# Block 0 of a state-space and gated feed-forward kernel: one copy moved to ScalarE, decay matmuls moved into two waits, loads placed anew

## The chip, the cores and the metric

The kernel runs on one core of a Trainium2 chip. The metric is the device time of one execution in microseconds. Engines are named as in the profile: PE is TensorE (matmul), PEld its weight loads, DVE is VectorE, ACT is ScalarE, POOL is GpSimd, SP is SyncE, which issues transfers.

## The reference

Two steps, the second on the result of the first. The first is a chunked linear recurrence over a sequence, for 4 batches x 8 heads, sequence 768, head size 32, state size 16:

```python
cum = np.cumsum(log_a)                       # within a chunk
M = (C @ B.T) * exp(cum_i - cum_j) * causal
y = M @ x + (C @ state) * exp(cum_i)
state = exp(sum(log_a)) * state + sum_j B_j x_j * exp(cum_last - cum_j)
```

The second takes y as 3072 tokens of 256 values, with weights of 256 x 1536 (gate and value) and 1536 x 256 (out):

```python
out = (np.maximum(y @ w_gate, 0.0) * (y @ w_val)) @ w_out
```

## The kernel before

The sequence of each batch is cut into chunks of 128 tokens, and two chunks are a pair: 12 pairs, three to a batch. The feed-forward step works on blocks of 512 tokens (two pairs): 6 blocks, NBLK. All is written in one order, and `in_order` (at the end) ties every engine to the order in which its instructions are written; each engine runs its own list and waits for the others by semaphores only.

A pair goes through these steps. The loads (`load`, or `held`, which first writes one element of the tile on DVE, so that the load isn't issued before DVE gets there) bring B, C and x. `dec_wide` makes the decay factors of a pair from the running products `cp`, by small fp32 matmuls; `late_decay` does so for pairs 2 and 3 into bank `d23`, and `decay` does all the others into `dall` (6 fp32 matmuls, L233), copied by ACT into `fac`. `scale` multiplies B by the reciprocal factors and C by the factors into `bs` (on POOL), and casts x into `xb`. `transp` (called through `turn`) transposes these on PE into `tp`; `bevac` and `cevac` (through `tevac`) copy out BT and two masked CT. `back` transposes BT back into bank `bt`, and `backevac` copies it to `bx`: B in the token order that the state needs. `G` makes C·B of the pair in four banks (8 matmuls, L364); `gevac` copies it to `gs` with the causal mask, partly by ACT casts (L377, L380) and POOL selects (L158), partly by DVE multiplies (L383, L385). `astep` adds one chunk to the state in `A_ps` (L397), and `sevac` copies it masked into `Sm` (L405). `inter` multiplies the state by C (L471) and `Dm` multiplies G by x (16 matmuls of 32 columns, L482), both into the bank of y (the tag `y`, of which there is one); `yevac` casts it into `yT`.

The feed-forward step has full tiles, `gv` (512 tokens of one of the NF = 12 slices of the hidden size: two matmuls for gate, two for value, ReLU on ACT at L514, product on DVE at L515 into `h`) and half tiles, `gvh` (256 tokens, L525, L528, L529), for which one pair's yT is enough. `fout` multiplies h by `wo` in four quarters of a block (L537), and `foevac` stores them. `keep_warm` writes filler matmuls of zeros into a tile of tag `y` that nobody reads.

G's four banks, bt, the tiles of gate and value, the output, `d23` and `dall` take turns in five shared PSUM banks (`bank`, NSHARED = 5): the n-th one waits until the (n-5)-th is copied out.

In block 0 nothing of the pairs ahead is ready, and the first pairs' steps stand between its half tiles. The order of before is half tiles 0 and 1 of pair 0's tokens, G and its copies, half tile 2, back and the copy bx on DVE, half tile 3, the decay of pairs 2 and 3, then `state`, `inter`, `Dm` and `yevac` of pair 1. The block's loop goes on with half tiles 4 and 5 of the first tokens, 0 to 5 of the second, and full tiles 6 to 11, with pair 2's steps between them, and `decay` at its end. The weights' slices 8 to 11 and `wo` are loaded by POOL's queue just ahead of half tile 3.

Of the kernel before, what the change touches and what calls it, by code (L numbers as in the profile page):

```python
# [29 lines left out]
def kernel(  # L30
# [35 lines left out]
    def bank(name="bank", shape=(128, 512), dtype=FP32):  # L66
        return mm.tile(list(shape), dtype, tag="shared", bufs=NSHARED, name=name)
# [174 lines left out]
    def new_bs(p):  # L242
        st[p]["bs"] = att.tile([128, 4, 128], BF16, tag="bs", name="bs", bufs=6)
        bs = st[p]["bs"]
        if p < NWIDE:
            st[p]["tin"] = [[bs[:, 2 * j + r] for r in range(2)] for j in range(2)]
        else:
            st[p]["tin"] = [[bs[:, 2 * i + j] for i in range(2)] for j in range(2)]
            st[p]["B"] = st[p]["tin"][0]
# [43 lines left out]
    def scale(p, eng):  # L293
        new_bs(p)
        scale_bc(p, eng)
        to_x(p, eng)
# [55 lines left out]
    def backevac(p, eng):  # L352
        s = st[p]
        bx = att.tile([128, 2, 128], BF16, tag="bx", name="bx", bufs=4)
        copy(eng, bx, s.pop("bt"))
        s["B"] = [bx[:, i] for i in range(2)]
# [44 lines left out]
    def sevac(p, i):  # L401
        if 2 * (p % PPB) + i == NC - 1:
            return
        S[2 * p + i + 1] = n = att.tile([128, 2, 128], BF16, tag="Sm", name="Sm", bufs=5)
        nc.vector.tensor_tensor(out=n, in0=A_ps[0], in1=smask, op=ALU.mult)  # L405

    def state(p, i):
        astep(p, i)
        sevac(p, i)
# [51 lines left out]
    def inter(p, i):  # L461
        s = st[p]
        y_bank(s)
        if 2 * (p % PPB) + i == 0:
            return
        Sm = S.pop(2 * p + i)
        for t in range(2):
            out = s["y"][t][:, i]
            if p < NWIDE:
                out = out.rearrange("s (r m) -> s r m", r=2)  # L470
            nc.tensor.matmul(  # L471
                out=out, lhsT=Sm[:, t], rhs=ct(p, i, t=t),
                start=opening(s, t), stop=False, skip_group_check=True)

    def Dm(p, apart=False):
        s = st[p]
        y_bank(s, apart)
        for t in range(2):
            for i in range(2):
                new = opening(s, t)  # L480
                for q in range(4):
                    nc.tensor.matmul(  # L482
                        out=s["y"][t][32 * q:32 * q + 32, i],
                        lhsT=s["x"][i][:, (4 * t + q) * D:(4 * t + q + 1) * D],
                        rhs=s["gs"][:, q, 2 * i + t],
                        start=new, stop=True,
                        tile_position=(0, 32 * q), skip_group_check=True)

    def yevac(p, *engs):
        s = st.pop(p)  # L490
        dst = yT[:, :, p * 256:(p + 1) * 256]
        if p >= NWIDE:
            copy(engs[0], dst.rearrange("q t (i m) -> q t i m", i=2), s["ya"])
            return
        for t in range(2):
            copy(engs[t % len(engs)],
                 dst[:, t].rearrange("q (i m r) -> q i r m", i=2, r=2),
                 s["y"][t].rearrange("q i (r m) -> q i r m", r=2))
# [15 lines left out]
        nc.scalar.activation(r, g, AF.Relu)  # L514
        nc.vector.tensor_tensor(out=fst[b][:, f], in0=r, in1=v, op=ALU.mult)  # L515

    def gvh(b, f, u):
        if f == 0 and u == 0:
            fst[b] = ffn.tile([128, NF, 512], BF16, tag="h", name="h")
        tk = slice(b * 512 + u * 256, b * 512 + (u + 1) * 256)  # L520
        fs = slice(f * 128, (f + 1) * 128)
        gv_ = bank("gv", (128, 2, 256))
        for j, w in ((0, wg), (1, wv)):
            for k in range(2):
                nc.tensor.matmul(out=gv_[:, j], lhsT=w[:, k, fs], rhs=yT[:, k, tk],  # L525
                                 start=(k == 0), stop=(k == 1), skip_group_check=True)
        r = ffn.tile([128, 512], BF16, tag="r", name="r", bufs=3)[:, 0:256]
        nc.scalar.activation(r, gv_[:, 0], AF.Relu)  # L528
        nc.vector.tensor_tensor(out=fst[b][:, f, u * 256:(u + 1) * 256], in0=r,  # L529
                                in1=gv_[:, 1], op=ALU.mult)  # L530

    def fout(b, ts):
        if ts % 2 == 0 or b == NBLK - 1:
# [48 lines left out]
    keep_warm(3)  # L582
    astep(0, 0)
    sevac(0, 0)
    new_bs(1)
    scale_bc(1, nc.vector, C_)

    def held(p):

        new_bc(p)  # L590
        nc.vector.memset(st[p]["bcr"][0:1, 0, 1, 0, 0:1], 0.0)
        load(p, nc.sync)
# [14 lines left out]
    def late_decay():  # L607
        d = bank("d23", (128, 2, 2, 8))
        for p in (2, 3):
            dec_wide(d[:, p - 2], p, p == 2)  # L610
        nc.scalar.copy(out=wfac[:, 2:4, 1], in_=d)
        nc.vector.reciprocal(wfac[:, 2:4, 0], d)

    def decay():
        d = bank("dall", (128, HC, 2, NB, 8))
        dec_all(d, range(HC))
        for w in range(2):
            cs = slice(w * HC, (w + 1) * HC)
            nc.scalar.copy(
                out=fac[:, :, cs, 1, :].rearrange("p b k h -> p k b h"), in_=d[:, :, w])  # L620
# [16 lines left out]
    gvh(0, 1, 0)  # L637
    G(1)
    gevac(1)
    gvh(0, 2, 0)  # L640
    back(1)
    backevac(1, nc.vector)
    weights(8, NF)
    weights_out(0, NF)
    gvh(0, 3, 0)
    late_decay()
    state(1, 0)
    inter(1, 0)
    inter(1, 1)
    Dm(1)  # L650
    state(1, 1)
    yevac(1, nc.scalar)

    for b in range(NBLK):
        P, Q, W = 2 * b + 2, 2 * b + 3, 2 * b + 1
        more = P < NPAIR
        for n in (P + 2, P + 3):
            if b and n < NPAIR:
                load(n, nc.sync)

        nh = 6 if b < 2 else 5
        for f in range(nh):
            if b == 0 and f < 4:
                continue
            gvh(b, f, 0)
            if b and f == (4 if b == 1 else 2):
                inter(W, 0)
                inter(W, 1)
                Dm(W)
                if b > 1 and more:  # L670
                    states(P)
                yevac(W, nc.scalar)
                if b > 1 and more:
                    spread(P)
        for f in range(nh):
            gvh(b, f, 1)
            if b == 1 and f in (0, 3):
                scale(P if f == 0 else Q, nc.gpsimd)
        for f in range(nh, NF):
            gv(b, f)  # L680
            if b == 0:
                if f == 6:
                    scale(P, nc.gpsimd)
                    for n in (3, 4, 5):
                        held(n)
                if f == 8:
                    turn(P)
                    tevac(P, nc.scalar, nc.vector)
                if f == 9:
                    back(P)  # L690
                    backevac(P, nc.vector)
                if f == 10:
                    state(P, 0)
                if f == 11:
                    scale(Q, nc.gpsimd)
                    state(P, 1)
            elif more:
                if f == (6 if b == 1 else 5):
                    turn(P)
                    tevac(P, nc.scalar, nc.vector)  # L700
                    if b > 1:
                        scale(Q, nc.gpsimd)
                if f == (9 if b == 1 else 8):
                    turn(Q)
                    tevac(Q, nc.scalar, nc.vector)
                    if Q + 1 < NPAIR:
                        scale(Q + 1, nc.gpsimd)
        if b == 0:
            decay()
        if more and b != 1:  # L710
            inter(P, 0)
            inter(P, 1)
        fout(b, 0)
        foevac(b, 0)
        if b == 1:
            states(P)
        if more:
            G(P)
        if b == 1:
            spread(P)  # L720
        if more:
            gevac(P)
        if b == 0:
            turn(Q)
            tevac(Q, nc.scalar, nc.vector)
        fout(b, 1)
        foevac(b, 1)
        if b == 0:
            back(Q)
            backevac(Q, nc.vector)  # L730
            for n in range(NB):
                nc.vector.reciprocal(fac[:, n, :, 0], fac[:, n, :, 1])
        fout(b, 2)
        foevac(b, 2)
        if more:
            if b == 1:
                inter(P, 0)
                inter(P, 1)
            Dm(P)
            states(Q)  # L740
            yevac(P, nc.scalar)
            G(Q)
            spread(Q)
            gevac(Q)
        fout(b, 3)
        foevac(b, 3)
# [32 lines left out]
```

## Time and profile before

| | |
|---|---|
| median of 3 runs | 131.5 us (131.4 to 131.59) |
| the profiled execution | 131.41 us, its span 129.7 us |
| busy: PE, DVE, ACT, POOL | 122.8, 94.1, 78.7, 42.3 us |
| half tile's matmul, 128x256, at 12 us and at 15 us | 421 ns, 272 ns |
| `dall`'s 6 matmuls | 28.19 to 29.07 us |
| first output matmul (L537) | 29.24 us |

Times in the profile are microseconds from the start of the span. A line of a timeline has the start, the time from first to last end, the engine, the line of the kernel, the operation and its tiles, the count, and in brackets how long the engine was idle before and who released it. The chain of work that ended last has the start, the length and the work, each piece being the one that the next one waited for.

### The profile page before, as it was taken

The page shows a single profiled execution, that of the slowest core. Times are in us where ns is not written, and L with a number is a line of the kernel's source. Part 1 is how long each engine was busy: PE and PEld are TensorE (multiplying, and loading weights), DVE is VectorE, ACT ScalarE, POOL GpSimd, SP SyncE. Part 2 cuts the span into 40 slices and gives each one's busy share as a digit, 9 for nine tenths or more (in the row PEclk, how much of TensorE's full clock was granted, in tenths as well). Part 3 has the DMA queues.
Part 4 walks back from the last instruction along what each step waited for, and adds up shares of the span by engine and source line. Part 5 has one row for each costly group of instructions (what it writes and reads, how often), then busy time and mean ns, then how long its engine had stood idle before and what let it go on. Part 6 is the DMA issues. An engine that isn't in the chain of part 4 may idle for free.

```text
span 129.7 us, 3374 instructions
## 1 busy us (share of the span) xinstructions
PE 122.8 (95%) x1253; PEld 84.9 (65%) x1260; DVE 94.1 (73%) x226; ACT 78.7 (61%) x175; POOL 42.3 (33%) x79
## 2 busy tenths in 40 slices
PE   6999879999999999999999999999999999999990
PEld 2555568547787557887467885477885577864770
DVE  4668769883986987579974888965898866597410
ACT  4062648744588864488744788745887645886410
POOL 7997392016193053261403523102800032000000
PEclk9999999999999999999999999999999999999999
DMA  3999999997999697259940289832200002200031
GB/s 70 146 185 161 175 134 145 190 156 79 121 117 214 70 130 110 81 107 120 110 73 0 86 133 134 95 55 81 81 5 0 0 0 86 81 0 0 5 104 58
DMA packets 71152, 11.98 MB, mean 92 GB/s; under 512 B 64864, under 2 KB 71072, under 8 KB 71136
## 3 DMA queue, kind: packets, MB, share of 16 engines
q1 hardware_dynamic: 63408, 8.49, 42.0%
q0 software_dynamic: 5360, 2.75, 16.6%
q10 hardware_dynamic: 2368, 0.52, 2.3%
q8 instruction: 10, 0.16, 0.5%
q14 instruction: 6, 0.05, 0.1%
HBM read 11.11 MB, written 3.15 MB: 110 GB/s over the span
## 4 chain that ended last, share of the span: by engine, by line
PE 84%; POOL 6%; DVE 4%; issue 2%; ACT 0%; POOLq 0%; DVEq 0%
PE o L537 25%; PE gv L525 22%; PE val L511 13%; PE gate L508 12%; PE y L482 4%; PE g L364 3%; PE tp L310 2%; PE y L471 2%; POOL bcr L86 1%; DVE h L515 1%; DVE gs L383 1%; POOL xb L168 1%; DVE h L529 1%; POOL wg L143 1%; PE A_ps L428 1%
## 5 line engine op out<-in xcount | busy, mean ns | idle before, releaser
L537 PE MATMUL o<-wo,h 128*128 128x256 bf16 x288 | 34.3, 273 | 0.0
L515 DVE TENSOR_TENSOR h<-r,val 128x512 bf16<-128x512 bf16 x40 | 27.3, 685 | 5.7 <-ACT r L514 2.2
L529 DVE TENSOR_TENSOR h<-r,gv 128x256 bf16<-128x256 bf16 x64 | 26.7, 421 | 6.1 <-ACT r L528 5.3
L537 PEld LDWEIGHTS <-h 128*128 128x128 bf16 x288 | 27.2, 98 | 5.3 <-issue 1.9
L514 ACT ACTIVATE r<-gate 128x512 bf16<-128x512 f32 x40 | 23.9, 597 | 8.1 <-PE gate L508 7.3
L528 ACT ACTIVATE r<-gv 128x256 bf16<-128x256 f32 x64 | 24.6, 384 | 4.2 <-PE gv L525 1.8
L525 PE MATMUL gv<-yT,wg 128*128 128x256 bf16 x128 | 25.1, 277 | 0.5 <-DVE h L529 0.5
L158 POOL TENSOR_SCALAR_AFFINE_SELECT gs<-gs 128x512 bf16<-128x512 bf16 (+1 forms) x24 | 12.2, 531 | 41.0 <-ACT gs L377 41.0
L525 PE MATMUL gv<-yT,wv 128*128 128x256 bf16 x128 | 24.9, 277 | 0.0
L511 PE MATMUL val<-yT,wv 128*128 128x512 bf16 x80 | 23.8, 379 | 0.3
L508 PE MATMUL gate<-yT,wg 128*128 128x512 bf16 x74 | 22.5, 379 | 0.0
L383 DVE TENSOR_TENSOR gs<-g,masks 128x512 bf16<-128x512 f32 x24 | 15.4, 684 | 5.4 <-PE g L364 5.4
L511 PEld LDWEIGHTS <-wv 128*128 128x128 bf16 x80 | 7.8, 98 | 9.4
L525 PEld LDWEIGHTS <-wg 128*128 128x128 bf16 x128 | 12.3, 99 | 2.6 <-issue 0.8
L525 PEld LDWEIGHTS <-wv 128*128 128x128 bf16 x128 | 12.7, 99 | 1.9 <-issue 0.2
L278 POOL TENSOR_TENSOR bs<-bcr,fac 128x256 bf16<-128x256 f32 x16 | 9.6, 620 | 12.0 <-DMA bcr<-in_B_dram 8.3
L252 ACT CAST yT<-y 128x512 bf16<-128x512 f32 (+1 forms) x15 | 7.4, 521 | 9.9 <-PE y L482 5.2
L377 ACT CAST gs<-g 128x512 bf16<-128x512 f32 x12 | 7.1, 589 | 8.9 <-PE g L364 8.9
L508 PEld LDWEIGHTS <-wg 128*128 128x128 bf16 x80 | 7.4, 98 | 5.6
L439 DVE TENSOR_TENSOR Sm<-A_ps,smask 128x256 bf16<-128x256 f32 x15 | 5.7, 415 | 6.5 <-PE A_ps L428 6.5
L553 ACT COPY ob<-o 128x512 f32<-128x512 f32 x10 | 5.9, 585 | 4.7 <-PE o L537 4.7
L252 POOL CAST xb<-xr 128x512 bf16<-128x512 f32 x11 | 6.8, 615 | 5.5 <-DMA xr<-in_x_dram 5.5
(79 smaller groups left out, 106.1 us busy)
## 6 DMA issues: line engine op xcount, KB each, us to landing
xr<-in_x_dram SPq DMA_DIRECT2D x21, 128.0 KB, 3.4
out_dram<-ob SPq DMA_DIRECT2D x10, 256.0 KB, 2.2
bcr<-in_C_dram SPq DMA_DIRECT2D x16, 64.0 KB, 3.1
bcr<-in_B_dram SPq DMA_DIRECT2D x16, 64.0 KB, 2.9
wg<-in_moe_w_gate_dram POOLq DMA_DIRECT2D x3, 256.0 KB, 4.4
wv<-in_moe_w_val_dram POOLq DMA_DIRECT2D x3, 256.0 KB, 4.8
wo<-in_moe_w_out_dram POOLq DMA_DIRECT2D x1, 768.0 KB, 9.8
bcr<-in_C_dram SPq DMA_DIRECT2D x3, 128.0 KB, 4.1
```

The lines of the kernel that those rows point to most:

```text
L158: nc.gpsimd.affine_select(out=dst, in_=dst, pattern=pattern, compare_op=ALU.is_ge, fill=0.0, base=0, channel_multiplier=-1)
L252: (eng.copy if eng is nc.scalar else eng.tensor_copy)(out=out, in_=in_)
L278: eng.tensor_tensor(out=dst[:, :, t], in0=src[:, :, t], in1=f[:, :, 4 * t:4 * t + 4].to_broadcast([128, n, 4, N]), op=ALU.mult)
L383: nc.vector.tensor_tensor(out=d[:, q], in0=g[q], in1=m, op=ALU.mult)
L508: nc.tensor.matmul(out=g, lhsT=wg[:, k, fs], rhs=yT[:, k, tk], start=(k == 0), stop=(k == 1))
L511: nc.tensor.matmul(out=v, lhsT=wv[:, k, fs], rhs=yT[:, k, tk], start=(k == 0), stop=(k == 1))
L514: nc.scalar.activation(r, g, AF.Relu)
L515: nc.vector.tensor_tensor(out=fst[b][:, f], in0=r, in1=v, op=ALU.mult)
L525: nc.tensor.matmul(out=gv_[:, j], lhsT=w[:, k, fs], rhs=yT[:, k, tk], start=(k == 0), stop=(k == 1), skip_group_check=True)
L528: nc.scalar.activation(r, gv_[:, 0], AF.Relu)
L529: nc.vector.tensor_tensor(out=fst[b][:, f, u * 256:(u + 1) * 256], in0=r, in1=gv_[:, 1], op=ALU.mult)
L537: nc.tensor.matmul(out=o[:, ts % 2], lhsT=fst[b][:, f, ts * 128:(ts + 1) * 128], rhs=wo[:, f], start=(f == 0), stop=(f == NF - 1), skip_gr ...
```

## The change

It is all in block 0. The copy `bx` of pair 1 goes from DVE to ACT, right behind G's casts. Half tiles 2 and 3 are split in two functions, so that their matmuls come ahead of pair 1's state step and their ReLU and product behind it. `decay` moves from the end of the block to the wait between pair 1's state and D, and its bank from the shared ones to the tag `tp`; `late_decay` moves behind D of pair 1, and the reciprocal is taken from the copied factors. Pair 1's yT is cast by ACT and DVE, one half each. The block has 4 half tiles for each pair and 8 full ones, in place of 6 and 6. Pair 2's scaling, transposes and state step come earlier, and loads 3, 4 and 5 are held at three places instead of one. Nine filler matmuls of 128 columns stand between pair 0's state step and its D.

```diff
+    def gvh_mm(b, f, u):            # the matmuls of gvh
...
+        fst[b, f, u] = gv_
+
+    def gvh_evac(b, f, u):          # ReLU and product of gvh
+        gv_ = fst.pop((b, f, u))
...
     astep(0, 0)
     sevac(0, 0)
+    keep_warm(9, 128)
     new_bs(1)
     scale_bc(1, nc.vector, C_)
...
         nc.scalar.copy(out=wfac[:, 2:4, 1], in_=d)
-        nc.vector.reciprocal(wfac[:, 2:4, 0], d)
 
     def decay():
-        d = bank("dall", (128, HC, 2, NB, 8))
+        d = mm.tile([128, HC, 2, NB, 8], FP32, tag="tp", name="dall")
...
     G(1)
     gevac(1)
-    gvh(0, 2, 0)
     back(1)
-    backevac(1, nc.vector)
+    backevac(1, nc.scalar)
+    gvh_mm(0, 2, 0)
+    gvh_mm(0, 3, 0)
     weights(8, NF)
     weights_out(0, NF)
-    gvh(0, 3, 0)
+    astep(1, 0)
+    sevac(1, 0)
+    gvh_evac(0, 2, 0)
+    decay()
+    inter(1, 0)
+    Dm(1)
+    inter(1, 1)
+    astep(1, 1)
+    yevac(1, nc.scalar, nc.vector)
+    gvh_evac(0, 3, 0)
     late_decay()
-    state(1, 0)
-    inter(1, 0)
-    inter(1, 1)
-    Dm(1)
-    state(1, 1)
-    yevac(1, nc.scalar)
+    held(3)
+    nc.vector.reciprocal(wfac[:, 2:4, 0], wfac[:, 2:4, 1])
+    sevac(1, 1)
+    scale(2, nc.gpsimd)
...
-        nh = 6 if b < 2 else 5
+        nh = (4, 6, 5)[min(b, 2)]
         for f in range(nh):
-            if b == 0 and f < 4:
+            if b == 0:
                 continue
...
             if b == 0:
+                if f in (5, 7):
+                    held(4 if f == 5 else 5)
                 if f == 6:
-                    scale(P, nc.gpsimd)
-                    for n in (3, 4, 5):
-                        held(n)
-                if f == 8:
                     turn(P)
                     tevac(P, nc.scalar, nc.vector)
-                if f == 9:
+                if f == 7:
                     back(P)
                     backevac(P, nc.vector)
-                if f == 10:
+                if f == 9:
                     state(P, 0)
-                if f == 11:
                     scale(Q, nc.gpsimd)
+                if f == 10:
                     state(P, 1)
...
-        if b == 0:
-            decay()
```

More of the change, by code (lines that the diff above doesn't have):

```diff
@@ L515, in gv @@
         nc.vector.tensor_tensor(out=fst[b][:, f], in0=r, in1=v, op=ALU.mult)
-    def gvh(b, f, u):
+    def gvh_mm(b, f, u):
         if f == 0 and u == 0:
@@ L530, in gvh @@
                                 in1=gv_[:, 1], op=ALU.mult)
+    def gvh(b, f, u):
+        gvh_mm(b, f, u)
+        gvh_evac(b, f, u)
     def fout(b, ts):
@@ L681 @@
             if b == 0:
+                if f in (5, 7):
+                    held(4 if f == 5 else 5)
                 if f == 6:
-                    scale(P, nc.gpsimd)
-                    for n in (3, 4, 5):
-                        held(n)
-                if f == 8:
                     turn(P)
                     tevac(P, nc.scalar, nc.vector)
-                if f == 9:
+                if f == 7:
                     back(P)
                     backevac(P, nc.vector)
+                if f == 9:
+                    state(P, 0)
+                    scale(Q, nc.gpsimd)
                 if f == 10:
-                    state(P, 0)
-                if f == 11:
-                    scale(Q, nc.gpsimd)
                     state(P, 1)
```

## The prediction

> **What bounds the kernel now.** I read the page first (busy time, then the slices), then the chain that ended last in order of time, then PE's timeline from 8 to 30 us, with ACT's and DVE's beside it, and last the transfers.
>
> ```profile
> PE 122.8 (95%) x1253; PEld 84.9 (65%) x1260; DVE 94.1 (73%) x226; ACT 78.7 (61%) x175; POOL 42.3 (33%) x79
> ```
>
> TensorE is the bound, with little left where it is full. So I looked for the stretch in which the chain leaves it:
>
> ```profile
> 10.43 0.87 PE y L482 x14
> ...
> 12.33 1.72 PE gv L525 x8
> 14.07 0.39 ACT r L528
> 14.49 0.42 DVE h L529
> 14.91 1.20 DVE gs L383 x2
> 16.11 0.33 DVE gs L385
> 16.44 0.33 DVE h L529
> 16.77 0.20 DVE bx L252
> 16.97 0.33 DVE h L529
> 17.30 0.27 DVE wfac L612
> 17.57 0.29 DVE Sm L405
> 17.90 0.28 PE y L471 x2
> ...
> 28.26 0.81 PE dall L233 x6
> ```
>
> From 14.07 to 17.90 the end is set by ACT and DVE, one instruction after the other: DVE masks G of pair 1 and does everything else behind it, the copy bx among it. From 18.5 on the chain is PE's almost throughout; there a step counts by its PE time, and `dall` is 0.81 us of it. PE's timeline shows the rest:
>
> ```profile
> 10.43 0.87 PE L482 MATMUL y<-gs,xb 128*32 128x128 bf16 x16 [0.19 <-POOL gs L158]
> ...
> 13.40 0.63 PE L525 MATMUL gv<-yT,wv 128*128 128x256 bf16 x2
> 13.97 0.52 PE L364 MATMUL g<-CT,BT 32*128 32x256 bf16 x8
> 14.96 0.38 PE L525 MATMUL gv<-yT,wg 128*128 128x256 bf16 x2 [0.48 <-DVE h L529]
> ...
> 27.12 0.28 PE L397 MATMUL A_ps<-xb,bx 128*128 128x256 bf16 x1 [0.23 <-DVE bx L252]
> ```
>
> Two matmuls of 128x256 take 0.63 us at 13.40 and 0.38 us at 14.96. In a run of them one starts every 0.213 us before 13.8 and every 0.109 us after: TensorE's pace doubles between 13.6 and 14.0, though the page's clock row stands at full for the whole span. That is about 3.5 us after D of pair 0 began at 10.43, and since then PE hardly paused.
>
> **The change, part by part.** The sum is made against the profiled execution: 131.41 us, of which 129.70 are the span; the runs' median is 131.5, 0.09 above.
>
> *The nine filler matmuls ahead of D of pair 0.* They write the tag-y bank that D's output also uses, so D waits for the last one. The first can start at about 10.16 (the filler before ends at 10.02, and D's weight load then started at 10.16). Cold 128-column fillers start 0.107 us apart: 0.96 us. The last takes 0.31, and with the same 0.14 D starts at 11.5, not 10.43. Its data are then all there: 11 of its matmuls took 0.44 us from 10.79 on, so 16 take 0.6, and inter follows at 12.1 instead of 11.23.
>
> What the fillers can bring is the pace. Before, PE stood from 10.02 to 10.43; now matmuls follow one another from the three fillers at 8.53 on. If the pace doubles 3.5 us after the start of an unbroken run, that is 12.0. I take this, since it is the only interval the trace shows. Then inter is done at about 12.3, the two casts at 12.78 (now 12.11, so +0.67), and the eight gv matmuls take 0.87 instead of 1.70. G of pair 1 is no longer behind them but behind DVE: Sm 0.41 and CT 0.61 after the cast (13.75), then h of the first half tile, whose bank G's fourth quarter takes (14.15). G ends at 14.55, against 14.49. The fillers and the faster pace cancel up to here.
>
> *bx on ACT.* ACT casts two parts of G (0.58 and 0.38) from 14.5 and copies bx at 15.45 to 15.83 (0.38, the row of BT). Now bx ends on DVE at 16.96. DVE's masking runs from 14.6 to 16.2, against 14.83 to 16.43.
>
> *Half tiles 2 and 3, A, decay, D, late decay.* PE's order becomes gv2, gv3, A, dall, inter, D, inter, A, d23. gv2 needs the bank of the first G quarter (15.1). gv3 needs that of the second, which DVE's last masking frees at 16.2; A, with bx ready, is queued behind gv3. So gv3 runs 16.25 to 16.69 (0.44 for a half tile), A to 16.80, dall (0.81) to 17.6, and Sm on DVE (17.05 to 17.4) hides under dall, where now PE waits 0.48 for it. Then 0.11 inter, 0.34 D, 0.11 inter, 0.11 A: 18.28. d23's 16 matmuls (16.16 to 16.83 now, in a wait) take 0.67: 18.95. The two casts of yT, split over ACT and DVE, need 0.22 + 0.45 after the second inter (18.85), so d23 covers them; without it PE would wait 0.6. The stream of gate and value tiles starts at 18.95 instead of 18.57: +0.38.
>
> *The stream.* Now 8 half tiles and 6 full ones (0.437 and 0.863 each: 8.67 us), after it 4 and 8 (8.65). dall is out of it: -0.81. Its work with turn, back and A (0.45) would end 9.12 after 18.57, at 27.69, but dall started at 28.19: 0.5 us stands idle, most of it at A of pair 2, which waited for bx. With turn two tiles and back two tiles earlier, bx is some 0.6 us ahead of A, and this goes: -0.5, with 0 as the other end if DVE falls behind. The last value tile's h must be done before the last matmul of the first output quarter, 1.2 us after it starts; relu and h take 1.3 from the last gate, so it is just hidden, where now dall gives 0.8 more room.
>
> *The loads and small steps.* Load 3 moves from 24.3 to about 19.6, 4 and 5 to two points of the stream. SP issues them and does nothing else then. The scaling of pair 2 moves behind the reciprocal (0.35 on DVE): POOL does it by 21.7 (1.2 and 0.6), and turn needs it at 23.3. The two fac copies on ACT (0.38) fall before yT's casts are ready. Zero for all these; the loads' risk is a rival.
>
> Sum: +0.38 - 0.81 - 0.5 - 0.02 = -0.95 us: 130.46, so 130.5. Behind block 0 nothing is changed and PE stays full; the gain should reach the end whole.
>
> **The rivals.**
>
> *The pace doubles no earlier than now.* If it is not the unbroken run that counts but fixed stretches of time, one ends near 13.9, and the one before it ended near 10.5, where only 0.35 us of the fillers have yet run. For it: eight fillers from 1.26 to 4.64 were an unbroken run of 3.4 us too, and the pace stayed. Price: gv runs from 12.98 cold until 13.9 and ends at 14.4, G ends at 14.97, masking at 16.7, gv3 at 17.2, and the stream starts at 19.45 (+0.88): 131.41 + 0.88 - 1.33 = 130.96, so 131.0. If, on the contrary, the stretch ending at 10.5 now passes, yT comes at 12.24, masking ends at 15.8, the stream starts at 18.53: 130.0.
>
> The Trainium skill, page "TensorE: Matmul & The Clock Gate", Part 1, "What's actually happening", says that the gate is opened by a busy window of about 3.4 us and that this window runs freely, not from the first matmul. By that page the fillers could bring nothing or the whole; the trace's eight early fillers agree that 3.4 us of matmuls alone are not enough.
>
> *The later stretch fails too.* D now comes after a pause of 0.4 us for the fillers' bank. If this keeps the pace low until 17.3, gv and G cost 0.5 more than in the rival above: 131.5.
>
> *wo comes late (the slower end).* This is the transfer in question, with the load that now starts beside it:
>
> ```profile
> wo<-in_moe_w_out_dram POOLq DMA_DIRECT2D x1, 768.0 KB, 9.8
> 24.34 0.37 SPq L86 DMA_DIRECT2D bcr<-in_C_dram  x1
> ```
>
> wo was issued at 17.50 and landed at 27.3; the first output matmul started at 29.24, and by the sum it starts at 28.3. Load 3 (0.52 MB) was issued at 24.34, beside wo's end; now it runs beside wo's whole length. At the 168 GB/s that the queues moved between 21 and 27 us, all of it ahead of wo is 3.1 us: landing at 30.4, a stall of 2.1, and 132.6. It decides from a landing later than 28.3. Against it: the wv part issued at 11.46 had load 2 beside it from 11.7 on and took 4.5 us, in the 4.5 to 5.0 of the others.
>
> **How the numbers follow.** Early pace, 130.0 to 130.8: 0.48. Pace as now, 130.8 to 131.4: 0.26. Both late, 131.5: 0.06. wo late, 131.8 to 132.8: 0.12. The rest, 0.08, is a price wrong by over 0.5 us that I do not see, mostly upwards, as the order on PE is now tight from 15 us on. A measurement of this kernel tells about 0.2%, 0.26 us, from no change: faster means below 131.24. From the first case 0.47 and from the second 0.14 lie there, with a trace of the rest: 0.62. Slower is above 131.76: wo late and the most of the rest, with the late pace's tail: 0.22. Between: 0.16. Range 129.9 to 132.1: it leaves out the far part of wo's delay and the lowest corner of the first case. The first case's own range is 130.0 to 130.8.
>
> **What would show it.** Right: 128x256 matmuls at 0.109 us apart by the first gv; bx on ACT by 15.9; Sm (L405) released with no PE wait, dall in its place; no PE wait for bx near A of pair 2; the first output matmul near 28.3. Wrong: gv of pair 0 still at 0.213 us (the fillers cost 1 us and bring nothing), a PE wait of the output matmul for wo, or a wait of gv3 longer than that for masking.

## The result, and the profile after

The changed kernel takes 129.69 us (4 runs, 129.5 to 130.14) against 131.51; the ratio is 0.9867, interval 0.984 to 0.9894. It is faster, by 1.8 us where 0.95 to 1.0 were forecast, and lies 0.2 below the range. Later runs of the kernel before lie in two groups with medians of 130.5 and 131.4; the first four all fell in the upper one. Why there are two is half of what follows. All medians and ranges from here on leave out disturbed runs, over 1.5% longer than the fastest of their kernel.

The busy times on the page after: TensorE has 1.5 us less work in a span 1.8 us shorter, so its share is as before.

```profile
PE 121.3 (95%) x1261; PEld 83.7 (65%) x1261; DVE 94.3 (74%) x224; ACT 78.5 (61%) x173; POOL 42.7 (33%) x79
```

The chain that ended last, after, over the stretch shown of before (start, length, work):

```profile
9.89 1.07 POOL gs L158 x2
11.68 0.44 PE tp L310 x4
12.54 0.61 DVE CT L332 x2
13.90 0.58 ACT gs L377
14.53 1.03 PE gv L525 x8
15.67 0.81 PE dall L233 x6
17.29 0.46 ACT yT L252
17.76 0.46 DVE yT L252
18.26 1.80 PE gv L525 x15
...
27.64 1.31 PE o L545 x12
```

The row of DVE pieces from 14.49 to 17.90 is gone: the chain crosses from ACT's cast of G to PE at 14.53, and `dall` stands in it at 15.67 in place of 28.26. PE's timeline, after:

```profile
8.16 0.81 PE L193 MATMUL w<-warm 128*128 128x512 bf16 x3
...
9.44 0.67 PE L193 MATMUL w<-warm 128*128 128x128 bf16 x9
10.64 0.71 PE L482 MATMUL y<-gs,xb 128*32 128x128 bf16 x16 [0.53 <-POOL gs L158]
...
12.04 0.38 PE L525 MATMUL gv<-yT,wg 128*128 128x256 bf16 x2
...
15.60 0.88 PE L233 MATMUL dall<-pick,cp 64*128 64x64 f32 x6
16.41 0.29 PE L471 MATMUL y<-CT,Sm 128*128 128x128 bf16 x2
...
25.41 0.27 PE L397 MATMUL A_ps<-xb,bx 128*128 128x256 bf16 x1
...
27.47 1.47 PE L545 MATMUL o<-wo,h 128*128 128x256 bf16 x12
```

Three things are to be seen. The first gv pair takes 0.38 us and not 0.63, so the pace was high before it; the three 512-column fillers at 8.16, ahead of everything that the change touches, already start 0.216 us apart (0.427 before). D of pair 0 at 10.64 waits for POOL, not for the nine fillers, which end at 10.11. And the state step of pair 2 (25.41) no longer waits for bx. The first output matmul starts at 27.47 against 29.24, 1.77 us earlier; from it to the end of the span it is 100.46 us in both.

### The profile page after: what moved, and what is told of

It reads as the page before. It is cut to its first block, busy times and chain, and to the rows that moved or that the text cites. A ratio compares the mean times of both kernels' runs of the same rounds, so it can differ in the third digit from the quotient of the medians.

```text
span 127.9 us, 3378 instructions
## 1 busy us (share of the span) xinstructions
PE 121.3 (95%) x1261; PEld 83.7 (65%) x1261; DVE 94.3 (74%) x224; ACT 78.5 (61%) x173; POOL 42.7 (33%) x79
## 4 chain that ended last, share of the span: by engine, by line
PE 86%; POOL 7%; issue 2%; DVE 1%; ACT 1%; POOLq 0%; DVEq 0%
PE o L545 25%; PE gv L525 21%; PE gate L508 14%; PE val L511 14%; PE y L482 3%; PE g L364 3%; PE tp L310 2%; PE y L471 2%; POOL wg L143 1%; POOL bcr L86 1%; POOL xb L168 1%; POOL gs L158 1%; PE A_ps L428 1%; PE dall L233 1%; POOL ident masks.py:199 1%
## 5 line engine op out<-in xcount | busy, mean ns | idle before, releaser
L515 DVE TENSOR_TENSOR h<-r,val 128x512 bf16<-128x512 bf16 x42 | 28.7, 686 | 5.6 <-ACT r L514 2.5
L514 ACT ACTIVATE r<-gate 128x512 bf16<-128x512 f32 x42 | 25.1, 597 | 8.2 <-PE gate L508 7.4
L533 DVE TENSOR_TENSOR h<-r,gv 128x256 bf16<-128x256 bf16 x60 | 25.1, 421 | 5.0 <-ACT r L532 4.1
L532 ACT ACTIVATE r<-gv 128x256 bf16<-128x256 f32 x60 | 23.1, 385 | 3.4 <-DVE wfac L666 0.6
L508 PE MATMUL gate<-yT,wg 128*128 128x512 bf16 x84 | 25.0, 379 | 0.0
L511 PE MATMUL val<-yT,wv 128*128 128x512 bf16 x84 | 25.0, 379 | 0.0
L525 PE MATMUL gv<-yT,wg 128*128 128x256 bf16 x120 | 23.3, 273 | 0.4 <-ACT gs L377 0.2
L525 PE MATMUL gv<-yT,wv 128*128 128x256 bf16 x120 | 22.9, 272 | 0.0
L511 PEld LDWEIGHTS <-wv 128*128 128x128 bf16 x84 | 8.2, 98 | 9.9
L525 PEld LDWEIGHTS <-wv 128*128 128x128 bf16 x120 | 11.7, 98 | 1.8 <-issue 0.5
L525 PEld LDWEIGHTS <-wg 128*128 128x128 bf16 x120 | 11.2, 98 | 2.2 <-issue 0.6
L508 PEld LDWEIGHTS <-wg 128*128 128x128 bf16 x84 | 7.8, 98 | 6.2
```

What stands on the lines that cost most here:

```text
L508: nc.tensor.matmul(out=g, lhsT=wg[:, k, fs], rhs=yT[:, k, tk], start=(k == 0), stop=(k == 1))
L511: nc.tensor.matmul(out=v, lhsT=wv[:, k, fs], rhs=yT[:, k, tk], start=(k == 0), stop=(k == 1))
```

## The experiments

Medians are of 5 to 12 runs. `before` ran beside each group, with medians of 131.0 to 131.4.

**When does the pace double?** Both kernels were profiled again, and the nine fillers were taken from the one and given to the other.

> The kernel before, unchanged, profiled a second time. The question is when TensorE's pace doubles, and whether that moment moves from run to run. Theory A (fixed stretches of 3.4 us that run freely, and a stretch counts or not by how full it is): the moment lies anywhere between about 6.5 and 14 us, and differs from the first profile's 13.9; where it is near 7, D of pair 0 still starts near 10.4 because it waits for POOL, and the time is 0.3 to 0.7 us less than 131.4. Theory B (an unbroken run of matmuls decides): 13.9 again, 131.4 to 131.6.

Measured: 131.37 us (130.35 to 131.94), in two groups. The profile by stretches (ends of the stretch, its length, PE's busy time and instructions, granted clock, DMA):

```profile
core 0: us, PE busy (x), PEclk, DMA share, GB/s
0.90:4.30 3.40, 3.04 (x8) 1.00 0.69 118
4.32:7.73 3.41, 2.33 (x32) 1.00 1.40 145
7.73:11.15 3.42, 2.90 (x27) 0.50 1.57 173
11.15:14.56 3.41, 3.41 (x34) 0.50 1.34 147
14.56:18.00 3.44, 2.50 (x34) 1.00 0.89 138
```

The clock was full from 4.32 us, half from 7.73 and full again from 14.56. (Before its first change the row shows 1.00 whatever the pace; the eight matmuls up to 4.3 started at the slow 0.427 us.) The changes are one and two times 3.41 us apart, so the moments lie on a fixed grid, and the grid lies elsewhere in each run: the first rise was at 13.96, 6.92, 4.32, 5.43, 5.63 and 6.55 us in the first six profiles. So the moment moves, as theory A says, and an unbroken run of matmuls does not decide. That the pace would rise as early as 4.3 and then fall back, neither theory had foreseen.

> The changed kernel, unchanged, profiled a second time. Its first profile has the doubled pace from 6.9 us on, before any instruction that the change touches. Theory A: the moment moves; with it near 14 the nine fillers hold D of pair 0 until about 11.5 and the time is near 131.0, with it near 7 it is 129.6. Theory B: 6.9 or at least before 12 again, 129.5 to 129.9.

Measured: 129.72 us (129.54 to 130.39), full clock from 5.43 us to the end. The time is that of an early rise; 5.43 alone, also before 12, would not tell the theories apart. One of the five runs, 130.39, has a mean granted clock of 0.987. One stretch of 3.41 us at half the pace takes 0.013 off the mean of a span of 130 us, so the pace probably fell back once in that run.

```diff
-    keep_warm(9, 128)
```

> The changed kernel without the nine filler matmuls. Theory A: the fillers bring nothing when the pace has doubled before them (D waits for POOL until 10.6 in any case): the same as the changed kernel within 0.2 us, 129.5 to 129.9; in a run with the late moment it is up to 0.9 faster than with them. The rival, that the fillers are what brings the early pace in most runs: 0.4 to 0.6 us slower than the changed kernel, 130.1 to 130.3.

Measured: 130.48 us (129.9 to 131.37), 0.8 slower than with the fillers: more than either expectation. The stretches of its profile, then two lines of its PE timeline:

```profile
core 0: us, PE busy (x) PEld busy (x) DVE busy (x) ACT busy (x) POOL busy (x), PEclk, DMA share, GB/s
5.63:9.04 3.41, 2.76 (x35) 1.49 (x35) 2.44 (x8) 1.76 (x5) 3.41 (x5) 1.00 1.29 145
9.05:12.46 3.41, 2.10 (x29) 1.29 (x29) 3.21 (x9) 1.16 (x4) 3.41 (x7) 1.00 1.85 171
12.46:15.87 3.41, 3.13 (x22) 1.79 (x21) 2.89 (x7) 2.01 (x7) 1.09 (x4) 0.50 1.25 180
```

```profile
12.26 0.44 PE L525 MATMUL gv<-yT,wv 128*128 128x256 bf16 x2
12.49 0.63 PE L525 MATMUL gv<-yT,wg 128*128 128x256 bf16 x2
```

The pace had doubled at 5.63 and fell back at 12.46, behind a stretch in which PE was busy for 2.10 of 3.41 us, and the half tiles that follow ran slow. So the fillers do not bring the pace, as the prediction had it, nor are they useless, as theory A had it here: they keep a pace that came earlier. The mean granted clock of the other runs agrees: it is 0.974 to 0.987 in seven of these eleven, and as low in two of the nine runs of the changed kernel.

```diff
     sevac(0, 0)
+    keep_warm(9, 128)
```

> The kernel before with the nine filler matmuls alone. Theory A: 131.2 to 131.6 where the pace has doubled early, up to 132.3 where it is late. The rival, that the fillers bring the early pace: 0.4 to 0.8 us faster than before, 130.7 to 131.1.

Measured: 130.69 us (130.47 to 131.52; ten of eleven runs from 130.47 to 130.87), full clock from 6.55 on. The fillers alone are worth 0.7 us to the kernel before; of its own 114 runs, 39 were below 131. Its profile shows the old order at the high pace:

```profile
11.97 0.38 PE L525 MATMUL gv<-yT,wg 128*128 128x256 bf16 x2
...
26.18 0.28 PE L397 MATMUL A_ps<-xb,bx 128*128 128x256 bf16 x1 [0.23 <-DVE bx L252]
...
28.30 1.47 PE L537 MATMUL o<-wo,h 128*128 128x256 bf16 x12
```

The first output matmul is at 28.30: of the 1.77 us between the two profiles, 0.93 are the pace and 0.83 the order.

**What the order's 0.83 us consist of.** One part undone at a time.

```diff
-    decay()                     # between the state step and D of pair 1
...
+        if b == 0:              # at the block's end, dall in a shared bank
+            decay()
```

> The changed kernel with decay back at the end of block 0 and its bank among the shared ones. By the prediction's sum dall is 0.81 us of full PE time there and covers a wait of 0.48 us for the state where it is now, of which 0.81 us of the changed kernel's span are spent between the state step and inter: 0.81 minus what PE saves at the wait (0.2 to 0.4, since D waits until 16.0 for G's select and Sm): 0.4 to 0.6 us slower, 130.1 to 130.3. The rival, that the place of dall counts for its whole time: 130.5.

Measured: 129.71 us (129.66 to 129.88): no difference, and both expectations missed. Two lines of PE's timeline before, then this kernel's:

```profile
17.90 0.28 PE L471 MATMUL y<-CT,Sm 128*128 128x128 bf16 x2 [0.48 <-DVE Sm L405]
18.11 0.41 PE L482 MATMUL y<-gs,xb 128*32 128x128 bf16 x16
```

```profile
15.18 0.27 PE L397 MATMUL A_ps<-xb,bx 128*128 128x256 bf16 x1
15.29 0.27 PE L471 MATMUL y<-CT,Sm 128*128 128x128 bf16 x2
15.49 0.41 PE L482 MATMUL y<-gs,xb 128*32 128x128 bf16 x16
15.97 0.28 PE L471 MATMUL y<-CT,Sm 128*128 128x128 bf16 x2
...
26.35 0.88 PE L233 MATMUL dall<-pick,cp 64*128 64x64 f32 x6
...
27.39 1.47 PE L545 MATMUL o<-wo,h 128*128 128x256 bf16 x12
```

Without dall, D of pair 1 starts 0.2 us after the half tiles and the state step, not 1.1 us. Before, the second `inter` stood ahead of D and waited 0.48 us for Sm. The change also puts D between the two, and here D runs from 15.49 to 15.90 while DVE copies Sm, from 15.49 to 15.91. So D alone fills nearly all of that wait, and dall has little left to hide: it costs its 0.81 us in either place. That D's new place is what took the wait away is read from the timeline; no run undoes it alone.

```diff
-    backevac(1, nc.scalar)
+    backevac(1, nc.vector)
```

> The changed kernel with the copy bx of pair 1 back on DVE. DVE masks until 15.57, so bx ends at 15.85 and not at 15.02; the state step starts at 15.9 and not at 15.39, and everything on PE behind it follows: 0.4 to 0.5 us slower, 130.1 to 130.2. The rival, that D waits for the late masking and the select in any case and takes the delay in: within 0.15 us, 129.6 to 129.9.

Measured: 130.18 us (129.88 to 130.48), 0.46 slower, as the first theory said. PE waits for it:

```profile
15.62 0.28 PE L397 MATMUL A_ps<-xb,bx 128*128 128x256 bf16 x1 [0.27 <-DVE bx L252]
```

```diff
-    held(3)                     # behind late_decay
...
-                if f in (5, 7):
-                    held(4 if f == 5 else 5)
                 if f == 6:
+                    for n in (3, 4, 5):
+                        held(n)
```

> The changed kernel with loads 3, 4 and 5 all held at full tile 6, as in the kernel before. Load 3 is then issued near 22.9 and not 18.57, so pair 3's scaling on POOL, which waits for bcr until 27.67 even so, would be near 28.5 to 29.5 and its transposes (29.21 now) 0.5 to 1.5 us later, with PE idle for it: 130.1 to 131.0. The rival, that wo lands earlier and all loads with it, since load 3 then runs beside less: no change, 129.6 to 129.8.

Measured: 130.17 us (129.89 to 131.47), 0.45 slower, at the low end of what was expected. On PE and on POOL:

```profile
29.61 0.40 PE L310 MATMUL tp<-ident,bs 128*128 128x128 bf16 x4 [0.19 <-POOL bs L278]
```

```profile
31.29 0.61 POOL L252 CAST xb<-xr 128x512 bf16<-128x512 f32 x1 [1.74 <-DMA xr<-in_x_dram]
31.86 1.04 POOL L158 TENSOR_SCALAR_AFFINE_SELECT gs<-gs 128x512 bf16<-128x512 bf16 x2
```

Pair 3's transposes wait 0.19 us, and pair 2's selects stand on POOL behind a cast that waits for x: 31.86, against 30.02 after the change. The loss lies behind the first output matmul, from which it is 100.93 us to the end of the span, against 100.46; that matmul starts at 27.62, only 0.15 later than after the change, though the clock rose at 10.31 in this run. With the loads left late, about half of what the order gains is lost.

**More fillers.**

```diff
-    keep_warm(6, 128)
+    keep_warm(8, 128)
...
-    keep_warm(4, 128)
+    keep_warm(5, 128)
...
-    keep_warm(9, 128)
+    keep_warm(13, 128)
```

> The changed kernel with more filler matmuls: 8 for 6 and 5 for 4 ahead of pair 0's transposes, 13 for 9 ahead of its D. Six profiles so far agree with two limits on how full a stretch of 3.41 us of PE is: the pace doubles behind one of 77% or more and halves behind one of 41% or less. By this theory the slow runs of the changed kernel (130.1 to 130.4) are runs in which an early stretch was too empty, and the fillers take them away: all runs at 129.5 to 129.8. The rival, that the slow runs have another cause, or that the fillers cost PE time where the pace is still low: 129.8 to 130.2, as wide as before.

Measured: 129.69 us (129.46 to 130.03), nothing to tell from the changed kernel's 129.69 and 129.72. One of the six runs, 130.03, still has a granted clock of 0.983, so the added fillers did not take all slower runs away.

**dall where PE does wait.** The wait for POOL ahead of pair 0's D was still filled with zeros. `decay` was moved there, out of its place ahead of pair 1's D.

```diff
-    keep_warm(9, 128)
+    decay()                     # e10: keep_warm(4, 128) ahead of it
```

> The changed kernel with decay in the place of the nine filler matmuls: dall's 0.81 us then lies in the wait of PE for POOL's select ahead of pair 0's D, which the profile of the changed kernel shows from 9.4 to 10.64 us, and in no place where PE sets the end. By the theory that dall has been on the path so far, at the state step as at the block's end: 0.8 us faster than the changed kernel, 128.9, if dall keeps PE's stretch full enough (over 41 to 49%); if not, the pace falls back in some runs and these are at 129.5 to 129.9. The rival, that dall is covered where it stands in the changed kernel: 129.6 to 129.8 or slower.

> The same with four filler matmuls ahead of decay. They end before D's data are there while the pace is high (four take 0.22 us), so they cost nothing then and fill the stretch: 128.8 to 129.0, with fewer runs in a slow group than without them. The rival, that dall is covered where it stands in the changed kernel: 129.6 to 129.8.

Measured: 129.67 us (129.05 to 130.89) and 129.57 (129.1 to 130.18): single runs at 129.1, no gain that stands out of the scatter. The first one's PE timeline says where it went:

```profile
26.28 0.39 PE L471 MATMUL y<-CT,Sm 128*128 128x128 bf16 x4
27.29 1.47 PE L545 MATMUL o<-wo,h 128*128 128x256 bf16 x12 [0.62 <-DMA wo<-in_moe_w_out_dram]
```

PE was done with the tiles a whole microsecond earlier than in the changed kernel, and stood until wo landed at 27.25. The pace took a part too: four of these eleven runs, at 129.8 to 130.9, have a granted clock of 0.968 to 0.987.

**Is wo the next bound?** The last weights, and so wo, were issued earlier, in three kernels.

```diff
     weights(4, 8, (1,))
+    weights(8, NF)              # from 12.4 us, ahead of G's selects on POOL
...
-    weights(8, NF)
     weights_out(0, NF)
```

> Decay ahead of pair 0's D with four fillers, as before, and the weights of slices 8 to 11 issued in POOL's idle stretch from 12.5 us, ahead of G's selects and not behind them, so that wo is issued 1.4 us earlier (15.4 and not 16.8). If wo's landing (26.7 to 27.2 in the two profiles with decay early, the first output matmul 0.04 us behind it) is what takes dall's 0.81 us: wo lands near 25.5 to 26.2, the first output matmul is at 26.4, and the time is 128.7 to 129.0. The rival, that the transfers as a whole are the limit (wo's queue only stands behind the others' bytes): wo lands as late as before, 129.3 to 129.9.

> The changed kernel with the same earlier weights. Its first output matmul stood 1.1 us behind wo's landing, so nothing to gain: 129.6 to 129.8. If the earlier weights delay load 2 or G's selects: 129.8 to 130.2.

> Decay at the block's end with the same earlier weights. Its PE is at dall until 27.16 whatever wo does, so nothing to gain: 129.6 to 129.8. A gain of over 0.3 us would say that wo held this kernel too.

Measured: 130.07 us (128.75 to 130.53), 130.25 (129.45 to 131.03) and 131.22 (130.26 to 131.73): 0.5, 0.5 and 1.5 above the same kernels with the weights in their old place. Only the last is clear of the scatter; none is faster. In the first one wo landed at 25.1, 1.6 us earlier than in the kernel with decay early and four fillers, and did no good:

```profile
22.76 0.40 PE L310 MATMUL tp<-ident,bs 128*128 128x128 bf16 x4 [0.98 <-POOL bs L278]
26.29 0.27 PE L397 MATMUL A_ps<-xb,bx 128*128 128x256 bf16 x1 [0.44 <-POOL xb L252]
```

```profile
21.51 1.19 POOL L278 TENSOR_TENSOR bs<-bcr,wfac 128x256 bf16<-128x256 f32 x2 [5.04 <-DMA bcr<-in_B_dram]
```

Load 2 came late in its place, and the first output matmul started at 28.35. In the third kernel the state step of pair 2 waits 1.12 us for the cast of load 2's x. Both theories missed a part: wo did land early, which the rival had denied, and the time did not follow it. That the transfers of block 0 as a whole are the next bound agrees with this; no run shows that no other order of the loads would do better.

**The order at the low pace.** All `keep_warm` calls taken out of both kernels.

> The changed kernel without any filler matmuls, early ones included. No stretch of 3.41 us before 12 us is then 77% full, so the pace doubles late, near 14 to 18 us, in all runs. By the theory of the pace: 130.8 to 131.5, as wide as the moment moves, and the comparison with the kernel before without fillers gives the order alone. The rival, that the pace matters little: 129.7 to 130.2.

> The kernel before without any filler matmuls. By the theory of the pace: at or above its usual upper group, 131.4 to 132.5, and 0.8 to 1.1 slower than the changed kernel without fillers, as with the early pace (130.72 against 129.72). The rival, that the order gains nothing while the pace is low, as the prediction's second case had it (0.4): 131.0 to 131.5.

Measured: 130.94 us (130.45 to 131.43) and 131.52 (131.28 to 132.05); the clock rose at 16.6 and 13.9 us. So the pace costs the changed kernel 1.2 us when it comes late, and the order alone is worth 0.6, less than at the high pace and more than the 0.4 of the prediction's second case. That the upper group of the kernel before (131.4) lies where it lies without fillers agrees with the pace as the cause of its two groups. So do the mean granted clocks of its later runs: all 39 below 131 have 0.998 or more, and of the 63 above, 55 have 0.974 to 0.987, that is one or two stretches at half the pace. The other eight may have risen late, which the mean does not show.

## Why the prediction was wrong, and where it was right

*The step that failed* is "If the pace doubles 3.5 us after the start of an unbroken run, that is 12.0". The interval was read from one profile, and it was chance that the grid's stretch and D of pair 0 began together there. The pace rose at 6.9, before the changed part, and the fillers' share is that it stayed. The term that follows from it, the start of the stream at +0.38, was mis-sized by 0.8 us: the first value matmul of the stream is at 18.37 against 18.79, so -0.42, and the stream's start counts as 18.15. That is the whole of the difference between 0.95 and 1.77, but not all of it is the pace: G ended 0.6 us earlier than forecast (13.94, not 14.55), half tile 3 gained another 0.7 because it did not wait for the masking, and 0.5 was given back. Of that, 0.3 went on the way from the state step to d23 (15.39 to 17.29), longer than reckoned, and the rest on the two casts of yT, which ran one after the other (17.29 to 18.21), so that PE waited for the second. The rival's last sentence came nearer (stream at 18.53, masking done at 15.8; measured 18.15 and 15.57, and 130.0 by its sum), for a stretch ending at 10.5 and not at 6.9. The range took its upper half from the rivals and cut the lower corner.

*The fillers' price.* A start of D at 11.5 was reckoned for the low pace. At the high one the nine start 0.056 us apart and take 0.5 us, and D, 0.21 later than before, waited for POOL.

*bx on ACT* was right in kind: done at 15.02 (15.83 forecast), worth 0.46 by the run that undid it. Its line on ACT:

```profile
14.63 0.39 ACT L252 COPY bx<-bt 128x256 bf16<-128x256 bf16 x1
```

That half tile 3 needs what DVE's last masking frees was a wrong reading: it started at 14.96, with the masking done at 15.57. The trace before had it already, with half tile 3 at 15.56 and that masking from 16.02 on. Which bank it took instead, the runs do not say.

*dall.* The sum had it rightly, without saying so: 0.81 gained at the end of the block and 0.81 lost within the +0.38. What was wrong was the wait of 0.48 us that it was to hide: in the prediction's own order D stands ahead of the second inter and fills that wait, so moving dall is worth nothing.

*The idle 0.5 us in the stream* went, as forecast: from its start to the first output matmul's inter it is 9.10 us after and was 9.62 without dall. The step at 25.41 has no wait.

*wo.* The rival did not happen: wo landed near 26.4, earlier than before. But it lay nearer than its 0.12 said: with dall out of the path, PE stood 0.62 us for it.

*Carried to the end.* 100.46 us from the first output matmul to the end of the span, before and after: right.

## What to carry to other kernels

Move a step into a wait only after asking whether another part of the same change already fills it; here D did, put ahead of the second inter, and the moved matmuls gained nothing. Early in a kernel, try fillers in TensorE's waits where they end before the data come: here they kept the pace in most runs and, once it was high, cost nothing. And take several runs and more than one profile before reading a moment of change as a rule: a kernel whose times form two groups may show only one of them in four runs.

## What the hardware showed

In these profiles the changes of TensorE's pace within one execution lie whole multiples of 3.41 us apart, and the grid lies differently in each execution: the first rise was anywhere from 4.3 to 16.6 us.

How full a stretch must be is known only roughly. The eight early fillers ran from 1.26 to 4.64 us. In the second profile of the kernel before, a stretch ended at 4.32; they covered 90% of it, and the pace rose. In the first, one ended at 3.72; they covered 72%, and it did not rise until 13.96.

The pace fell back behind stretches in which the profile counts PE busy for 2.10 us (no nine fillers), 2.33 (second profile of before) and 2.72 (decay at the end, earlier weights), but stayed behind one with 2.50 (second profile of before). So this busy time alone does not give the limit. Counted from the matmuls' starts, as columns divided by the pace, the three held about 33 to 43% of a stretch, depending on how the small fp32 matmuls are counted, and the emptiest that kept the pace 40 to 44%. This is an estimate, as are the 77% and 41% that one expectation names, and no sharp limit.

The Trainium skill, page "TensorE: Matmul & The Clock Gate", Part 1, has the freely running window of about 3.4 us, and the grid seen here agrees. It gives the fall as what follows an idle window; here a stretch in which PE was busy for 2.10 of 3.41 us was enough, and the measurement decides.
